# Odd head pairs on swapped halves of a bank of their own, and QK in 64x64 tiles

## The chip, the core and the metric

One core of a Trainium2 chip runs the whole program. The metric is device time in microseconds (us), from the first to the last instruction of one execution. Before the change it is 432.07 us, the median of three runs (430.96 to 432.35).

## What is computed

Three layers follow one another: decayed linear attention (retention), a soft mixture of experts, and a bilinear layer.

```python
scores = q @ k.T / sqrt(64)                    # 8 batches, 8 heads, 576 positions, 64 features
x = (scores * gamma_h ** (i - j) * (i >= j)) @ v   # -> 4608 tokens x 512 features
logits = x @ phi                               # 32 slots, 8 experts of 4
slots = softmax(logits, over tokens).T @ x     # 32 x 512
slot_out[e] = relu(slots[e] @ w1[e]) @ w2[e]   # 8 experts, 512 -> 1024 -> 512
x = softmax(logits, over slots) @ slot_out
out = (((x @ m1) * (x @ m2)) @ w3) @ w_out
```

## The kernel before

**Units.** The 4608 tokens are worked through as 36 units of 128 tokens. An item (g, c) takes the sequences g and g + 4 and 128 positions of each (c = 0 to 3); its two units, x = 0 and 1, are one sequence each. The item c = 4 is a single unit, the tail, with the last 64 positions of both sequences. So each of the four groups g has nine units: two with c = 0, six with c = 1 to 3, one tail.

**Heads.** A unit has four head pairs p. Pair p holds head h = 0 on SBUF partitions 0 to 63 (`lo`) and head h = 1 on partitions 64 to 127 (`hi`), with the 64 features along the partitions. The result `xts` has the same order: feature rows of pair p, tokens along the free axis.

**The steps of a unit on TensorE**, each a burst of fp32 matmuls. An fp32 matmul that isn't a transpose stands in the profile as two MATMUL records; "rows*columns" is the part of the 128x128 array that it takes.

- `emit_kt` (L201): four 128*128 transposes of the scaled keys into a miscellaneous bank; ScalarE copies it to `kt` (L202).
- `emit_qk` (L229): eight matmuls, 64*128, keys stationary, 128 query columns moving; head 0 goes to bank 0, head 1 to bank 1. The tail uses 64*64 (L224).
- `emit_p` on VectorE (L239, two instructions): bank 0 and 1 times the causal mask, into `pm`.
- `emit_pv` (L257): eight matmuls, 128*64, adding v x pm to the unit's result bank. The tail uses 64*64 (L250).
- `emit_state` (L270): eight matmuls, 128*64, adding k x v to the running state in bank 4; ScalarE copies it out after each item.
- `emit_inter` (L290): eight matmuls, 64*64, state x q, that start the unit's result bank; only where c > 0. In the tail sixteen, with 64 moving columns.
- `emit_xt` on VectorE (L303, L299 in the tail): the result bank times a table of decays, into `xts`.
- `emit_xtr` (L315): four transposes of `xts`, four units later; every fourth unit also `emit_logits` (L325, 16 matmuls, 128*32) and `emit_slots` (L409).

The result bank of a unit is whole: all four pairs, head 0 on partitions 0 to 63 and head 1 on 64 to 127, as the inputs lie. Odd and even units take turns between two banks:

```python
def xt_view(u):
    return bank[(5, 3)[u % 2]].rearrange("p (k t) -> p k t", k=4)
```

**Order.** Nothing is scheduled automatically; each engine runs its instructions in the order in which the loop writes them. Iteration u of the unit loop writes: key scaling for unit u + 4 (GpSimd L188, ScalarE L193), keys' transposes of u + 3, PV of u, state of u + 1, QK and mask of u + 2, `emit_xt` of u, inter of u + 1, next transfers, transposes of unit u - 4, softmax pieces, and between them the conversion of the weights of the last layer in five steps a piece (VectorE L465, L467, L459; ScalarE L464, L466; GpSimd L485). All transfers are issued by SyncE (SP) in program order; SP waits in order for a buffer to become free.

**Before the loop** SP issues the small tables and the first keys, queries and values (L609 to L621); `kr` are raw keys, scaled into `k`. VectorE L643 and GpSimd L649 build the decay tables from `xtab_sb` and `stab_sb`.

**After the loop** the buffers of the units are filled with expert weights (`in_ew`, 64 tiles of 512 KB, L544); the eight experts run on them (L553, L572) beside the product of w3 and w_out (L526). Then come the pairwise tables (L943) and the output stage (L1006 to L1011).

Of the kernel before, what the change touches and what calls it, by code (L numbers as in the profile page):

```python
# [31 lines left out]
def retention_softmoe_bilinear(  # L32
# [76 lines left out]
    even = tabs_sb[:, 196:197]  # L109
    ptail = tmp.tile([128, 256], F32, tag="h0", name="ptail").rearrange("p (k i) -> p k i", k=4)  # L110
# [96 lines left out]
    def xt_view(u):  # L207
        return bank[(5, 3)[u % 2]].rearrange("p (k t) -> p k t", k=4)
# [7 lines left out]
    def emit_qk(u):  # L216
        Q = q_tile(u)
        x = units[u][1]
        if tail(u):
            ps = qk_view(0).rearrange("p (x k i) -> p x k i", x=2, k=4)  # L220
            for x in range(2):
                for p in range(4):
                    for h, a in halves:
                        nc.tensor.matmul(out=ps[a, x, p], lhsT=Q[a, 1, x, p], rhs=Q[a, 0, x, p], start=True, stop=True)  # L224
            return
        for p in range(4):
            for h, a in halves:
                ps = qk_view(h).rearrange("p (k c i) -> p k c i", k=4, c=2)
                nc.tensor.matmul(out=ps[:, p], lhsT=ktb[u % 2][a, p], rhs=Q[a, :, x, p], start=True, stop=True)  # L229
# [13 lines left out]
    def emit_pv(u):  # L243
        x = units[u][1]
        if tail(u):
            V = vb[units[u][0] % VBUF][:, 0:512].rearrange("p (x k j) -> p x k j", x=2, k=4)
            for x in range(2):
                for p in range(4):
                    for h, a in halves:
                        nc.tensor.matmul(  # L250
                            out=xt_view(u)[a, p, 64 * x:64 * x + 64], lhsT=V[a, x, p], rhs=p_tail(u)[a, x, p],
                            start=False, stop=True, skip_group_check=True,
                        )
            return
        for p in range(4):
            for h, a in halves:
                nc.tensor.matmul(  # L257
                    out=xt_view(u)[a, p], lhsT=v_tile(u)[:, 1 - h, x, p], rhs=p_main(u)[:, h, p],
                    start=(block_of(u) == 0 and p == 0), stop=True, skip_group_check=True,
                )  # L260
# [21 lines left out]
    def emit_inter(u):  # L282
# [4 lines left out]
        for y in range(2) if tail(u) else (x,):  # L287
            for p in range(4):
                for h, a in halves:
                    nc.tensor.matmul(  # L290
                        out=xt_view(u)[a, p, 64 * y:64 * y + 64] if tail(u) else xt_view(u)[a, p].rearrange("p (c i) -> p c i", c=2),
                        lhsT=S[a, y, p], rhs=Q[a, 0, y, p] if tail(u) else Q[a, :, x, p],
                        start=(p == 0 and (y == 0 or not tail(u))), stop=True, skip_group_check=True,
                    )

    def emit_xt(u):
        v4 = lambda t: t.rearrange("p k (x i) -> p k x i", x=2)
        if tail(u):
            nc.vector.tensor_tensor(  # L299
                out=v4(xts[u % 6]), in0=v4(xt_view(u)), in1=xtab_sb[0][:, :, 0:64].unsqueeze(2).to_broadcast([128, 4, 2, 64]), op=ALU.mult,  # L300
            )
        else:
            nc.vector.tensor_tensor(out=xts[u % 6], in0=xt_view(u), in1=xtab_sb[block_of(u)], op=ALU.mult)  # L303
# [301 lines left out]
    with tc.manual_schedule():  # L605
# [9 lines left out]
        nc.sync.dma_start(out=xtab_sb[0][:, :, 0:64], in_=tabs[:, 328:584].rearrange("p (k i) -> p k i", k=4))  # L615
# [5 lines left out]
        nc.sync.dma_start(out=phi_sb, in_=phi)  # L621
# [7 lines left out]
        for n in (512, 512, 128):  # L629
# [14 lines left out]
            out=xtab_sb[0][:, :, 64:128], in0=xtab_sb[0][:, :, 0:64], in1=stab_sb[:, 1].unsqueeze(2).to_broadcast([128, 4, 64]), op=ALU.mult,  # L644
# [3 lines left out]
        for c in range(1, 4):  # L648
            nc.gpsimd.tensor_tensor(out=xtab_sb[c], in0=xtab_sb[0], in1=stab_sb[:, 2 * c].unsqueeze(2).to_broadcast([128, 4, 128]), op=ALU.mult)  # L649
# [17 lines left out]
        for u in range(NU):  # L667
# [11 lines left out]
            emit_pv(u)  # L679
            if u + 1 < NU:  # L680
# [4 lines left out]
            emit_xt(u)  # L685
# [93 lines left out]
        for k in range(4):  # L779
            nc.tensor.matmul(out=sT[:, k], lhsT=acc[:, 128 * k:128 * k + 128], rhs=ib, start=True, stop=True)  # L780
# [309 lines left out]
```

## Time and profile before

| | |
|---|---|
| median of three runs | 432.07 us |
| the profiled execution's own time | 432.36 us |
| its span (first to last instruction) | 430.6 us |
| TensorE matmul busy | 408.1 us, 95% of the span |
| VectorE, ScalarE, GpSimd busy | 57%, 46%, 39% |
| DMA | 47968 packets, 108.15 MB, 251 GB/s on average |
| granted TensorE clock | full from slice 1 to 40 |

Read it by stage: up to about 191 us the unit loop, from there to about 281 us the experts, then tables and the output stage. "Busy" counts a record from its modelled start to its modelled end, so a busy TensorE may still be filling, draining or running half of its array. Where a burst's length matters, take the distance from its start to the start of the next burst.

### The profile page before, as it was taken

The numbers are of one execution on the slowest core, as the hardware profiler recorded it, in microseconds if no ns is written. First come the engines' busy times: TensorE is split into PE (matmuls) and PEld (weight loads), VectorE is DVE, ScalarE is ACT, GpSimd is POOL, SyncE is SP. The second block draws the span as 40 slices with busy tenths as digits, with TensorE's granted clock in tenths as the row PEclk, the third lists the DMA queues.
The fourth block names the chain that finished last, engine by engine and source line by source line (L and its number), as shares of the span: only waits on it lengthen the run. The fifth ranks groups of instructions, "written<-read, shape, count | busy, mean of one in ns | idle before, by whom it ended". The sixth has DMA issues, their size and how long they took to land.

```text
span 430.6 us, 10442 instructions
## 1 busy us (share of the span) xinstructions
PE 408.1 (95%) x4211; PEld 312.0 (72%) x4211; DVE 246.2 (57%) x456; ACT 198.0 (46%) x415; POOL 166.6 (39%) x149
## 2 busy tenths in 40 slices
PE   5999898999899999999999988899999999999996
PEld 3888787888788777786556544356888888888884
DVE  3356677787677676654587556228964434443420
ACT  2233775665546555552455433123444445444431
POOL 0521666543425333431354333102745344434410
PEclk9999999999999999999999999999999999999999
DMA  5986798689677884869999999969054988879733
GB/s 157 362 298 241 259 330 287 178 286 349 241 221 244 294 282 161 299 198 352 393 354 413 408 410 408 401 166 189 1 132 89 231 216 201 209 198 231 188 79 93
DMA packets 47968, 108.15 MB, mean 251 GB/s; under 512 B 7376, under 2 KB 10064, under 8 KB 47920
## 3 DMA queue, kind: packets, MB, share of 16 engines
q1 hardware_dynamic: 47920, 107.49, 78.0%
q8 instruction: 33, 0.54, 0.5%
q14 instruction: 15, 0.12, 0.1%
HBM read 96.85 MB, written 10.62 MB: 250 GB/s over the span
## 4 chain that ended last, share of the span: by engine, by line
PE 76%; DMA 18%; ACT 2%; SPq 1%; DVE 1%; issue 1%; DVEq 0%; ACTq 0%
PE bank L229 9%; PE bank L1006 8%; PE bank L1007 8%; PE bank L1008 8%; PE bank L257 8%; DMA k<-in_ew 7%; PE bank L290 7%; DMA kt<-in_ew 5%; PE bank L943 5%; PE bank L201 4%; PE bank L315 4%; PE bank L270 4%; DMA v<-in_ew 2%; DMA xts<-in_ew 2%; PE bank L526 2%; PE bank L1009 2%
## 5 line engine op out<-in xcount | busy, mean ns | idle before, releaser
L597 POOL TENSOR_TENSOR cc<-mw_sb,cc 128x512 fp32r<-128x512 f32 x36 | 46.8, 1310 | 55.9 <-ACT cc L596 55.9
L239 DVE TENSOR_TENSOR pm<-bank,msb 128x512 f32<-128x512 f32 x64 | 41.2, 686 | 44.4 <-PE bank L229 44.4
L485 POOL TENSOR_TENSOR vals<-vals,msb 128x512 int32<-128x512 int32 x24 | 30.7, 1280 | 66.7 <-DVE vals L459 44.2
L526 PE MATMUL bank<-wop,w3p 128*128 128x512 f32 x192 | 50.4, 405 | 0.0
L595 DVE TENSOR_TENSOR mw_sb<-lga,raw 128x512 f32<-128x512 f32 x32 | 30.0, 958 | 35.3 <-POOL cc L597 28.0
L316 ACT COPY xg<-bank 128x512 f32<-128x512 f32 x34 | 20.0, 587 | 64.4 <-PE bank L315 64.4
L1011 ACT ACTIVATE mw_sb<-bank,rz 128x512 f32<-128x512 f32 x36 | 24.8, 689 | 49.8 <-PE bank L1009 28.6
L526 PEld LDWEIGHTS bank<-wop,w3p 128*128 128x128 f32 x192 | 34.2, 188 | 14.9 <-issue 8.7
L1006 PE MATMUL bank<-w3p,cc 128*128 128x512 f32 x108 | 42.4, 392 | 0.0
L1007 PE MATMUL bank<-w3p,cc 128*128 128x512 f32 x108 | 42.2, 391 | 0.0
L1008 PE MATMUL bank<-w3p,cc 128*128 128x512 f32 x108 | 42.2, 391 | 0.0
L229 PE MATMUL bank<-q,kt 64*128 64x128 f32 x512 | 39.6, 295 | 0.8 <-DVE pm L239 0.8
L485 POOL TENSOR_TENSOR mw_sb<-mw_sb,msb 128x512 int32<-128x512 int32 x16 | 20.3, 1270 | 47.7 <-DVE mw_sb L459 24.5
L229 PEld LDWEIGHTS bank<-q,kt 64*128 64x128 f32 x512 | 33.2, 196 | 3.8 <-DVE pm L239 1.1
L257 PE MATMUL bank<-pm,v 128*64 128x128 f32 x512 | 35.0, 279 | 0.0
L495 POOL TENSOR_TENSOR w3p<-vals,w3p 128x512 fp32r<-128x512 f32 x16 | 20.5, 1282 | 33.8 <-ACT w3p L490 33.8
L257 PEld LDWEIGHTS bank<-pm,v 128*64 128x64 f32 x512 | 27.3, 136 | 5.4 <-issue 5.4
L188 POOL TENSOR_TENSOR k<-kr,msb 128x512 f32<-128x512 f32 (+1 forms) x30 | 24.4, 835 | 17.6 <-DMA kr<-in_v 14.3
L290 PE MATMUL bank<-q,st 64*64 64x128 f32 (+1 forms) x512 | 30.6, 261 | 0.0
L201 PE MATMUL bank<-cst,k 128*128 128x128 f32 x128 | 21.4, 294 | 8.5 <-ACT lga L352 6.8
L466 ACT ACTIVATE msb<-raw 128x512 int32<-128x512 uint32 x40 | 27.8, 696 | 0.0
L596 ACT CAST cc<-mw_sb 128x512 fp32r<-128x512 f32 x36 | 21.6, 618 | 13.0 <-DVE mw_sb L595 10.4
(191 smaller groups left out, 784.1 us busy)
## 6 DMA issues: line engine op xcount, KB each, us to landing
q<-in_q SPq DMA_DIRECT2D x20, 512.0 KB, 5.6
raw<-expt SPq DMA_DIRECT2D x36, 256.0 KB, 4.4
kr<-in_v SPq DMA_DIRECT2D x16, 512.0 KB, 5.0
v<-in_v SPq DMA_DIRECT2D x16, 512.0 KB, 6.1
raw<-in_m SPq DMA_DIRECT2D x16, 512.0 KB, 6.2
raw<-in_w SPq DMA_DIRECT2D x16, 512.0 KB, 6.0
out_x<-mw_sb SPq DMA_DIRECT2D x64, 128.0 KB, 2.7
k<-in_ew SPq DMA_DIRECT2D x14, 512.0 KB, 10.2
```

The source lines that it names most:

```text
L201: nc.tensor.transpose(ps[:, 128 * p:128 * p + 128], k_tile(u)[:, x, p].rearrange("p h j -> p (h j)"), ident)
L229: nc.tensor.matmul(out=ps[:, p], lhsT=ktb[u % 2][a, p], rhs=Q[a, :, x, p], start=True, stop=True)
L239: nc.vector.tensor_tensor(out=p_main(u)[:, h], in0=qk_view(h).rearrange("p (k t) -> p k t", k=4), in1=mask_sb.unsqueeze(1).to_broadcast([1 ...
L257: nc.tensor.matmul(out=xt_view(u)[a, p], lhsT=v_tile(u)[:, 1 - h, x, p], rhs=p_main(u)[:, h, p], start=(block_of(u) == 0 and p == 0), stop ...
L290: nc.tensor.matmul(out=xt_view(u)[a, p, 64 * y:64 * y + 64] if tail(u) else xt_view(u)[a, p].rearrange("p (c i) -> p c i", c=2), lhsT=S[a, ...
L485: nc.gpsimd.tensor_tensor(out=ti, in0=ti, in1=parts[j % 2].bitcast(I32), op=ALU.add)
L526: nc.tensor.matmul(out=ps, lhsT=x, rhs=y, start=(k8 == 0 and part == 0), stop=(k8 == 7 and part == 2))
L595: eng.tensor_tensor(out=e, in0=x, in1=y[:, m], op=ALU.mult)
L597: nc.gpsimd.tensor_tensor(out=cl[m], in0=e, in1=ch[m], op=ALU.subtract)
L1006: nc.tensor.matmul(out=ob, lhsT=ch[m][:, sl], rhs=gh[m], start=(m == 0), stop=False)
L1007: nc.tensor.matmul(out=ob, lhsT=ch[m][:, sl], rhs=gl[m], start=False, stop=False)
L1008: nc.tensor.matmul(out=ob, lhsT=cl[m][:, sl], rhs=gh[m], start=False, stop=False)
```

## The change

Heads of odd pairs (p = 1, 3) now leave TensorE on the other half of the partitions, into bank 3, and even pairs go to bank 5, in every unit. So the 64x64 tiles of `emit_inter` (and of the tail's PV) use, in turn, all four quarters of the array: rows lo to columns lo, hi to hi, lo to hi, hi to lo. `emit_qk` is cut into twice as many matmuls, each with 64 of the 128 key columns, in the same four quarters. Both result banks are used by each unit, so `emit_xt` becomes two VectorE instructions of half the size and stands straight behind PV. What depends on the row order of odd pairs follows: the decay table, a second position table `xstab`, `phi`, and the slots' transposition `sT`.

```diff
+    xstab = tabs_sb[:, 200:236].rearrange("p (c k) -> p c k", c=9)
-    def xt_view(u):
-        return bank[(5, 3)[u % 2]].rearrange("p (k t) -> p k t", k=4)
+    def xt_view(p):
+        return bank[(5, 3)[p % 2]][:, 128 * (p // 2):128 * (p // 2) + 128]
+
+    def side(p, h):
+        return (lo, hi)[h ^ (p % 2)]
...
-                nc.tensor.matmul(out=ps[:, p], lhsT=ktb[u % 2][a, p], rhs=Q[a, :, x, p], start=True, stop=True)
+                for b in (lo, hi):
+                    nc.tensor.matmul(out=ps[b, p], lhsT=ktb[u % 2][a, p, b], rhs=Q[a, :, x, p], start=True, stop=True)
...
-                    out=xt_view(u)[a, p], lhsT=v_tile(u)[:, 1 - h, x, p], rhs=p_main(u)[:, h, p],
-                    start=(block_of(u) == 0 and p == 0), stop=True, skip_group_check=True,
+                    out=xt_view(p)[side(p, h)], lhsT=v_tile(u)[:, 1 - h, x, p], rhs=p_main(u)[:, h, p],
+                    start=(block_of(u) == 0 and p < 2), stop=True, skip_group_check=True,
...
     def emit_xt(u):
...
+        for r in range(2):
+            ps = bank[(5, 3)[r]][:, 0:256].rearrange("p (k t) -> p k t", k=2)
+            o, f = xts[u % 6][:, r::2], xtab_sb[block_of(u) % 4][:, r::2]
...
+            nc.vector.tensor_tensor(out=o, in0=ps, in1=f, op=ALU.mult)
...
-        nc.sync.dma_start(out=xtab_sb[0][:, :, 0:64], in_=tabs[:, 328:584].rearrange("p (k i) -> p k i", k=4))
+        for r in range(2):
+            for a, b in ((lo, hi), (hi, lo)) if r else ((slice(0, 128),) * 2,):
+                nc.sync.dma_start(out=xtab_sb[0][a, r::2, 0:64], in_=tabs[b, 328:584].rearrange("p (k i) -> p k i", k=4)[:, r::2])
+                nc.sync.dma_start(out=xstab[a, :, r::2], in_=tabs[b, 292:328].rearrange("p (c k) -> p c k", c=9)[:, :, r::2])
...
-        nc.sync.dma_start(out=phi_sb, in_=phi)
+        for r in range(2):
+            for a, b in ((lo, hi), (hi, lo)) if r else ((slice(0, 128),) * 2,):
+                nc.sync.dma_start(out=phi_sb[a, r::2], in_=phi[b, r::2])
...
             emit_pv(u)
+            emit_xt(u)
             if u + 1 < NU:
                 emit_state(u + 1)
             if u + 2 < NU:
                 emit_qk(u + 2)
                 emit_p(u + 2)
-            emit_xt(u)
             if u + 1 < NU:
                 emit_inter(u + 1)
...
         for k in range(4):
-            nc.tensor.matmul(out=sT[:, k], lhsT=acc[:, 128 * k:128 * k + 128], rhs=ib, start=True, stop=True)
+            for a, b in ((lo, 64), (hi, 0)) if k % 2 else ((slice(0, 128), 0),):
+                n = a.stop - a.start
+                nc.tensor.matmul(out=sT[a, k], lhsT=acc[:, 128 * k + b:128 * k + b + n], rhs=ib, start=True, stop=True)
```

The tables that `emit_xt` and the loops before it read come from `xstab` in place of `stab_sb`; the line numbers of the changed kernel are a few higher (QK L234, inter L295, PV L262, state L275, mask L244, `emit_xt` L308).

TensorE before, one iteration of the loop with c > 0, from the keys' transposes on (bank_67 and bank_68 are banks 0 and 1, bank_72 is bank 5, bank_70 bank 3, bank_71 the state):

```order
L201 MATMUL bank_69<-cst,k_111 128x128 x4
L257 MATMUL bank_72<-pm_97,v_105 64x128 x8
L270 MATMUL bank_71<-v_105,k_110 64x64 x8
L229 MATMUL bank_67<-q_103,kt 128x128
L229 MATMUL bank_68<-q_103,kt 128x128
...
L290 MATMUL bank_70<-q_102,st 64x128 x8
L201 MATMUL bank_73<-cst,k_109 128x128 x4
L257 MATMUL bank_70<-pm_98,v_105 64x128 x8
```

The same iteration of the changed kernel:

```order
L202 MATMUL bank_69<-cst,k_111 128x128 x4
L262 MATMUL bank_72<-pm_97,v_105 64x128 x2
L262 MATMUL bank_70<-pm_97,v_105 64x128 x2
...
L275 MATMUL bank_71<-v_105,k_110 64x64 x8
L234 MATMUL bank_67<-q_103,kt 64x128 x2
L234 MATMUL bank_68<-q_103,kt 64x128 x2
...
L295 MATMUL bank_72<-q_102,st 64x128 x2
L295 MATMUL bank_70<-q_102,st 64x128 x2
...
L202 MATMUL bank_73<-cst,k_109 128x128 x4
```

QK stands as 16 matmuls in place of eight, and inter writes both result banks, where before it wrote the bank that the unit ahead of it had not used.

VectorE before, from the mask of one unit to the mask of the next, in an iteration with logits:

```order
L239 TENSOR_TENSOR pm_98<-bank_67,msb 128x512
L239 TENSOR_TENSOR pm_98<-bank_68,msb 128x512
L303 TENSOR_TENSOR xts_92<-bank_70,xtab_84 128x512
L465 TENSOR_SCALAR mw_sb<-mw_sb 128x512
L331 TENSOR_REDUCE mt<-bank_69 128x1
L336 TENSOR_TENSOR mn<-mt,mn 128x1
L338 TENSOR_SCALAR nm<-mn 128x1
L467 TENSOR_SCALAR mw_sb<-mw_sb 128x512
L459 SCALAR_TENSOR_TENSOR mw_sb<-raw,mw_sb 128x512
L239 TENSOR_TENSOR pm_97<-bank_67,msb 128x512
```

and of the changed kernel:

```order
L308 TENSOR_TENSOR xts_92<-bank_72,xtab_84 128x2x128
L308 TENSOR_TENSOR xts_92<-bank_70,xtab_84 128x2x128
L244 TENSOR_TENSOR pm_98<-bank_67,msb 128x512
L244 TENSOR_TENSOR pm_98<-bank_68,msb 128x512
L470 TENSOR_SCALAR mw_sb<-mw_sb 128x512
L336 TENSOR_REDUCE mt<-bank_69 128x1
...
L464 SCALAR_TENSOR_TENSOR mw_sb<-raw,mw_sb 128x512
L308 TENSOR_TENSOR xts_93<-bank_72,xtab_84 128x2x128
L308 TENSOR_TENSOR xts_93<-bank_70,xtab_84 128x2x128
L244 TENSOR_TENSOR pm_97<-bank_67,msb 128x512
```

The two halves of `emit_xt` moved from behind the mask to ahead of it, and so behind the conversion steps of the unit before.

SP before, from the first values to the second keys (msb holds the position tables, slotm the decay table):

```order
L177 DMA v_104<-in_v 128x2x512
L615 DMA slotm<-in_tabs 128x4x64
L161 DMA kr_108<-in_v 128x2x512
```

and of the changed kernel:

```order
L178 DMA v_104<-in_v 128x2x512
L622 DMA slotm<-in_tabs 128x2x64
L623 DMA msb<-in_tabs 128x18x1
L622 DMA slotm<-in_tabs 64x2x64
L623 DMA msb<-in_tabs 64x18x1
L622 DMA slotm<-in_tabs 64x2x64
L623 DMA msb<-in_tabs 64x18x1
L162 DMA kr_108<-in_v 128x2x512
```

Six table transfers stand where one did; a "18x1" one consists of single fp32 elements.

## Rows read from the trace of the kernel before

**Rows 1.** Stretches: TensorE, its loads, VectorE, ScalarE, GpSimd, clock, DMA share, GB/s

```profile
10.80:24.60 13.80, 13.02 (x159) 11.53 (x158) 6.08 (x9) 4.21 (x10) 8.01 (x9) 1.00 1.02 331
80.00:100.00 20.00, 20.00 (x346) 16.98 (x346) 15.96 (x29) 12.46 (x30) 9.48 (x9) 1.00 0.71 239
220.00:240.00 20.00, 20.00 (x158) 10.79 (x156) 14.82 (x35) 8.12 (x18) 9.48 (x8) 1.00 1.02 400
```

**Rows 2.** The page's chain that ended last, by engine

```profile
PE 76%; DMA 18%; ACT 2%; SPq 1%; DVE 1%; issue 1%; DVEq 0%; ACTq 0%
```

**Rows 3.** The same chain in order of time, from the loop's last units on

```profile
190.59 1.10 PE bank L250 x32
192.09 8.73 DMA k<-in_ew
200.88 9.46 DMA xts<-in_ew
```

**Rows 4.** TensorE in order of time: start, us, instruction, count

```profile
83.42 1.09 PE L290 MATMUL bank<-q,st 64*64 64x128 f32 x16
84.45 0.66 PE L315 MATMUL bank<-cst,xts 128*128 128x128 f32 x4
85.03 1.08 PE L325 MATMUL bank<-xts,cst 128*32 128x128 f32 x32
86.04 1.09 PE L257 MATMUL bank<-pm,v 128*64 128x128 f32 x16
86.97 0.63 PE L270 MATMUL bank<-v,k 128*64 128x64 f32 x16
87.53 1.16 PE L229 MATMUL bank<-q,kt 64*128 64x128 f32 x16
88.62 1.09 PE L290 MATMUL bank<-q,st 64*64 64x128 f32 x16
```

**Rows 5.** TensorE around a tail's QK

```profile
92.15 1.15 PE L224 MATMUL bank<-q 64*64 64x64 f32 x32
93.14 1.04 PE L290 MATMUL bank<-q,st 64*64 64x128 f32 x16
94.11 0.66 PE L315 MATMUL bank<-cst,xts 128*128 128x128 f32 x4
```

**Rows 6.** VectorE in order of time, the stretch of rows 4

```profile
83.53 1.29 DVE L239 TENSOR_TENSOR pm<-bank,msb 128x512 f32<-128x512 f32 x2 [1.22 <-PE bank L229]
84.73 0.68 DVE L303 TENSOR_TENSOR xts<-bank,xtab 128x512 f32<-128x512 f32 x1
85.33 1.49 DVE L465 TENSOR_SCALAR mw_sb<-mw_sb 128x512 f32<-128x512 f32 x1
...
87.77 0.69 DVE L459 SCALAR_TENSOR_TENSOR mw_sb<-raw,mw_sb 128x512 uint32<-128x512 uint32 x1
```

**Rows 7.** VectorE groups by form: busy us, mean ns

```profile
L857 DVE COPY acc<-bank 128x256 f32<-128x256 f32 x1 | 0.4, 424 | 5.0 <-ACT acc L856 5.0
```

**Rows 8.** All engines in order of time, start of the loop

```profile
13.85 1.79 POOL L188 TENSOR_TENSOR k<-kr,msb 128x512 f32<-128x512 f32 x2 [11.59 <-DMA kr<-in_v]
...
17.36 1.52 PE L201 MATMUL bank<-cst,k 128*128 128x128 f32 x8
```

**Rows 9.** Source lines L177 and L615, first issue of each: start, issue to landing

```profile
L177 SPq DMA_DIRECT2D v<-in_v x1: 607/607/607, 5.9 to 5.9; - x1
...
DMA to landing us min/median/max: 6.0/6.0/6.0
...
L615 SPq DMA_DIRECT2D slotm<-in_tabs x1: 604/604/604, 6.6 to 6.6; - x1
...
DMA to landing us min/median/max: 5.8/5.8/5.8
```

**Rows 10.** Transfers by line: issues, size of each, median us to landing

```profile
msb<-in_tabs SPq DMA_DIRECT2D x4, 4.0 KB, 2.3
...
expt<-et SPq DMA_DIRECT2D x8, 16.0 KB, 1.6
```

More of the change, by code (lines that the diff above doesn't have):

```diff
@@ L250, in emit_pv @@
                         nc.tensor.matmul(
-                            out=xt_view(u)[a, p, 64 * x:64 * x + 64], lhsT=V[a, x, p], rhs=p_tail(u)[a, x, p],
+                            out=xt_view(p)[side(p, h), 64 * x:64 * x + 64], lhsT=V[a, x, p], rhs=p_tail(u)[a, x, p],
                             start=False, stop=True, skip_group_check=True,
@@ L290, in emit_inter @@
                     nc.tensor.matmul(
-                        out=xt_view(u)[a, p, 64 * y:64 * y + 64] if tail(u) else xt_view(u)[a, p].rearrange("p (c i) -> p c i", c=2),
+                        out=xt_view(p)[side(p, h), 64 * y:64 * y + 64] if tail(u) else xt_view(p)[side(p, h)].rearrange("p (c i) -> p c i", c=2),
                         lhsT=S[a, y, p], rhs=Q[a, 0, y, p] if tail(u) else Q[a, :, x, p],
-                        start=(p == 0 and (y == 0 or not tail(u))), stop=True, skip_group_check=True,
+                        start=(p < 2 and (y == 0 or not tail(u))), stop=True, skip_group_check=True,
                     )
     def emit_xt(u):
[L297 to L303, printed above, removed]
+        for r in range(2):
+            ps = bank[(5, 3)[r]][:, 0:256].rearrange("p (k t) -> p k t", k=2)
+            o, f = xts[u % 6][:, r::2], xtab_sb[block_of(u) % 4][:, r::2]
+            if tail(u):
+                o, ps = (t.rearrange("p k (x i) -> p k x i", x=2) for t in (o, ps))
+                f = f[:, :, 0:64].unsqueeze(2).to_broadcast([128, 2, 2, 64])
+            nc.vector.tensor_tensor(out=o, in0=ps, in1=f, op=ALU.mult)
     L = {"cc": []}
@@ L643, in retention_softmoe_bilinear @@
         nc.vector.tensor_tensor(
-            out=xtab_sb[0][:, :, 64:128], in0=xtab_sb[0][:, :, 0:64], in1=stab_sb[:, 1].unsqueeze(2).to_broadcast([128, 4, 64]), op=ALU.mult,
+            out=xtab_sb[0][:, :, 64:128], in0=xtab_sb[0][:, :, 0:64], in1=xstab[:, 1].unsqueeze(2).to_broadcast([128, 4, 64]), op=ALU.mult,
         )
@@ L648, in retention_softmoe_bilinear @@
         for c in range(1, 4):
[L649 removed]
+            nc.gpsimd.tensor_tensor(out=xtab_sb[c], in0=xtab_sb[0], in1=xstab[:, 2 * c].unsqueeze(2).to_broadcast([128, 4, 128]), op=ALU.mult)
         emit_qk(1)
```

## The prediction

> **What bounds the kernel now.** I read the stretches first, then the chain of waits, then both engines' order of time inside one unit, and last the start, where the change adds transfers.
>
> In the unit loop TensorE is never idle: 20.00 of 20 us from 80 to 100 us, at a granted clock of 1.00, while the DMA share is 0.71 [rows 1]. After the loop the limit is another one: from 220 to 240 us the DMA share is 1.02 at 400 GB/s. The chain says the same, TensorE with 76% and DMA with 18% of the span [rows 2]; its first long DMA pieces begin at 192.09 us, right behind the loop's last burst at 190.59 [rows 3], because those expert tiles go into buffers that the loop gives back at its end. So what the loop saves moves the whole expert stream forward, and I carry it to the end at full value.
>
> **How long a burst takes, and why.** The distance between the starts of two bursts is what counts [rows 4]. PV, 16 records with 128 columns on two column halves, takes 86.04 to 86.97 = 0.93 us; state, the same shape with 64 columns, 0.56; QK 87.53 to 88.62 = 1.09; inter 83.42 to 84.45 = 1.03. Two records run side by side, so PV is eight steps. Four unknowns fit all of these: a step of 128 columns, 0.109 us; one of 64 columns, 0.058; a first weight load, 0.05, which nothing covers; and 0.10 for emptying the array where the next burst has another tile shape. PV: 8 x 0.109 + 0.05 = 0.92, with no change of shape before state. State: 8 x 0.058 + 0.10 = 0.56. Inter: 0.87 + 0.05 + 0.10 = 1.02. QK's 128-column loads make its first load 0.12. The proof of the last term is the tail: its QK has inter's shape, and there inter takes 93.14 to 94.11 = 0.97 in place of 1.03, and QK itself 0.99 = 16 x 0.058 + 0.05, without the 0.10 [rows 5].
>
> **The change, part by part.**
>
> *Inter.* Eight matmuls of 128 columns on two quarters are eight steps; on four quarters four steps. No row shows four quarters at once. The nearest rows show each half of it: PV runs two column halves on the same rows side by side, QK two row halves, and logits (L325) four column strips, 32 records in 1.01 us, eight steps [rows 4]. I take four at a time. Inter then costs 4 x 0.109 + 0.10 = 0.54. Of 24 full inters 20 stand behind a full QK: 1.03 - 0.54, and as the first load now hides behind QK of the same shape, I count 0.48 each; 4 stand behind a tail's QK, 0.97 - 0.54 = 0.43. Together 9.6 + 1.7 = 11.3 us.
>
> *QK.* Twice the matmuls, half the columns, four at a time: still eight steps. It gains the smaller first load (0.07), and 0.10 more where inter follows in the same shape. That is 23 units x 0.17 and 9 x 0.07, 4.5 us.
>
> *Tails.* Four inters of 16 x 0.058 + 0.15 = 1.08 would become 8 x 0.058 + 0.10 = 0.56, four PVs (1.10 [rows 3]) 0.61: 4 x 0.52 + 4 x 0.49 = 4.0 us if records can start every 15 ns. The fastest long burst shown is logits, 0.109 / 4 = 27 ns a record; at that rate 32 records still take 0.87 and the gain is 0.6 us. I take 2.2, about the middle.
>
> Sum for TensorE: 18.0 us, between 16.4 and 19.8 by the tails.
>
> *A new wait.* Inter of unit u + 1 now writes the banks that `emit_xt` of u reads; before, they alternated. So VectorE has to reach `emit_xt` and finish it before QK of u + 2 ends. Two 128x256 instructions take 0.424 us each [rows 7], overlapping by the 0.08 that the two mask instructions show (1.29 for two of 0.69 [rows 6]): 0.76 us against 0.68 today. Behind inter stand the transposes and PV, so all of TensorE waits. Walk through the stretch shown: the mask starts at 83.53, and without L303 behind it L465 (1.49 us here) starts 0.6 earlier, so the last conversion step ends at 87.77 + 0.69 - 0.6 = 87.86 and `emit_xt` at 88.6. QK would start 0.48 earlier than 87.53, last 0.92 and end at 87.97: inter is 0.6 us late. That is a unit with logits and a slow L465; a unit has spare time otherwise, for VectorE has 4 us of 20 idle [rows 1]. I count four such units, 2.5 us, with 0 and 28 x 0.3 = 8.4 as ends.
>
> *The start.* The six table transfers contain 2304 + 2 x 1152 = 4608 pieces of 4 bytes, ahead of the second keys, queries and values. The DMA engines are full there, share 1.02 [rows 1]. Nothing shows 4-byte pieces. One end: the decay table's 512 pieces of 256 bytes, issued at 6.6, landed at 12.4, behind the values at 5.9 + 6.0 = 11.9, so 0.5 us, 1.0 ns a piece [rows 9]: 4.6 us. The other: 256 pieces of 16 bytes land in 2.3 us, where another small transfer of 32 pieces lands in 1.6 [rows 10]; 0.7 us / 224 is 3.1 ns a piece: 14.4 us. The first is nearer in load, the second in size; I take 1.2 ns, 5.5 us, as full queues are what the new pieces meet. GpSimd waits for exactly these keys (11.59 us, until 13.85) and has them scaled at 15.64; TensorE transposes them at 17.36 [rows 8]. So 1.7 us are spare, and 3.8 are a stall, once: later loads are two and three items ahead. Ends 1 and 12.7. SP's five further issues of 0.6 us run under the queue's backlog, for the values take 6.0 us from issue to landing [rows 9].
>
> *At no cost.* `phi` in three pieces is needed 25 us later. The two extra matmuls of `sT` come while the chain waits for expert tiles (192 to 210 us [rows 3]); without that cover they cost about 0.1 us.
>
> **Sum.** 18.0 - 2.5 - 3.8 = 11.7 us. The profiled execution took 432.36 us, 0.29 more than the median; against the median I predict 420.4 us.
>
> **Rivals.**
>
> *Slower: weight loads of two quarters on the same rows do not run beside a matmul on those rows.* Then a step is 0.109 + 0.05 = 0.16. QK becomes 1.33 (1.43 with emptying): 23 x 0.24 + 9 x 0.34 = 8.6 us lost; inter 0.74: 24 x 0.29 = 7.0 won. With the start's 3.8 that is 5.4 us more, 437.5 us. The change loses from a step of 0.145 us on. For it speaks that no row has four quarters. Against it: PV's two column halves share all rows and still step in 0.109 [rows 4]. [...] 10%.
>
> *VectorE paces the loop.* Between 80 and 100 us it is busy 15.96 of 20 [rows 1]; with 0.08 more a unit and the loop a tenth shorter that is over 90%, in strict order, with two waits for TensorE in each unit. If each of 28 inters comes 0.3 late: 420.4 + 5.9 = 426.3 us. 10%.
>
> *The start is dear.* At 3.1 ns a piece: 432.07 - 18.0 + 2.5 + 12.7 = 429.3 us. 10%.
>
> **How the numbers follow.** The forecast itself has 70%. Its best corner is 19.8 won, 1 lost at the start and none on VectorE, 413.3 us; its poor one 16.4 won, 7.5 and 5 lost, 428.2. The range 413.3 to 428.5 holds nearly all of it and VectorE's rival; it leaves out the slower rival and half of the dear start. About 0.3% (1.3 us) is what a measurement of this kernel can tell from no change. Faster by more: the forecast and two rivals, less the meeting of two poor cases, 0.87. Slower: 0.10. Between: 0.03.
>
> **What would show it.** Inter's bursts 0.54 us apart from the next, QK 0.92 before inter. About 512 more MATMUL records. The packet count up by some 5000. TensorE's transposes of the second keys at about 21 us in place of 17.36. A new line in the waits: TensorE's inter behind `emit_xt`, a few us in all, mostly in units with logits. The expert stream full from about 180 us, and the stage behind the loop as long as before. It is wrong if QK's bursts grow beyond 1.1 us, if inter waits in every unit, or if the loop ends 12 us earlier and the experts do not.

## The result, and the profile after

The changed kernel takes 425.92 us (425.62 to 430.72 in four runs) where the kernel before, on the same chip, takes 431.67 (430.96 to 432.35): a ratio of 0.9891, with an interval of 0.9856 to 0.9926. It is faster, by 5.75 us. 420.4 us were forecast, so a little less than half of the forecast gain of 11.7 us came.

The profiled execution took 425.71 us, with a span of 424.0 where before it was 430.6. The page's first and third parts, and its row of the granted clock:

```profile
PE 393.7 (93%) x4727; PEld 297.3 (70%) x4727; DVE 252.0 (59%) x492; ACT 198.2 (47%) x415; POOL 167.6 (40%) x149
PEclk9589999999999999999999999999999999999999
DMA packets 53076, 108.24 MB, mean 255 GB/s; under 512 B 12608, under 2 KB 15168, under 8 KB 53024
q8 instruction: 37, 0.61, 0.6%
```

TensorE has 516 records more and the queues 5108 packets more than before, as announced. In the row of the clock the second of the forty slices (10.6 to 21.2 us) fell to 0.5 and the third to 0.8. The last row is a queue that the forecast never looked at: TensorE's instructions, 37 fetches of 16 KB, before 33.

The stretches of [rows 1], now:

```profile
10.80:24.60 13.80, 9.10 (x104) 7.55 (x106) 3.48 (x7) 1.30 (x4) 4.60 (x5) 0.51 0.82 197
80.00:100.00 20.00, 19.54 (x403) 15.64 (x396) 17.07 (x36) 12.54 (x30) 10.65 (x10) 1.00 0.80 252
220.00:240.00 20.00, 20.00 (x152) 12.07 (x151) 12.25 (x31) 9.33 (x22) 8.30 (x7) 1.00 1.02 407
```

Three readings. In the start TensorE does 9.10 us of work instead of 13.02, and its granted clock is 0.51 instead of 1.00. That figure alone doesn't give TensorE's speed there: the first two QKs take 2.08 and 2.67 us in the kernel before, at 1.00, and 1.99 and 2.57 now, at 0.50; later ones take 1.16 and 1.10. In the loop VectorE went from 15.96 to 17.07 of 20, and TensorE now idles 0.46 us. Behind the loop nothing changed.

An undisturbed unit is what the forecast said. TensorE in order of time (start, duration), as in [rows 4]:

```profile
29.43 1.10 PE L234 MATMUL bank<-q,kt 64*64 64x128 f32 x32
30.35 0.62 PE L295 MATMUL bank<-q,st 64*64 64x128 f32 x16
30.90 0.66 PE L202 MATMUL bank<-cst,k 128*128 128x128 f32 x4
```

QK to inter is 0.92, inter to the next burst 0.55; 0.92 and 0.54 were forecast. The whole unit, from one PV's start to the next, takes 3.55 us, before 4.19. Around a tail, the counterpart of [rows 5]:

```profile
55.60 0.64 PE L295 MATMUL bank<-q,st 64*64 64x64 f32 x32
56.17 0.66 PE L320 MATMUL bank<-cst,xts 128*128 128x128 f32 x4
...
57.30 0.69 PE L255 MATMUL bank<-pm,v 64*64 64x64 f32 x32
57.93 0.69 PE L275 MATMUL bank<-v,k 128*64 128x64 f32 x16
```

32 small matmuls in 0.57 and in 0.63 us, 18 to 20 ns each. The forecast had hesitated between 15 and 27 ns and had taken half of the tails' gain; all of it came.

So where did five microseconds go? First, the start. Before (see also [rows 8]), the issues of the second and third keys and unit 1's PV:

```profile
7.21 0.61 SPq L161 DMA_DIRECT2D kr<-in_v  x1
...
11.97 0.64 SPq L161 DMA_DIRECT2D kr<-in_v  x1
...
21.97 1.09 PE L257 MATMUL bank<-pm,v 128*64 128x128 f32 x16
```

Now, all engines in order of time:

```profile
7.86 4.10 SPq L622 DMA_DIRECT2D slotm<-in_tabs  x1
...
14.07 0.72 SPq L162 DMA_DIRECT2D kr<-in_v  x1
...
19.43 1.61 POOL L189 TENSOR_TENSOR k<-kr,msb 128x512 f32<-128x512 f32 x2 [17.18 <-DMA kr<-in_v]
20.25 0.63 SPq L162 DMA_DIRECT2D kr<-in_v  x1
21.10 1.97 PE L202 MATMUL bank<-cst,k 128*128 128x128 f32 x8 [3.84 <-POOL k L189]
23.00 1.79 PE L262 MATMUL bank<-pm,v 128*64 128x128 f32 x16
27.35 0.66 PE L202 MATMUL bank<-cst,k 128*128 128x128 f32 x4 [1.07 <-POOL k L189]
27.94 1.09 PE L262 MATMUL bank<-pm,v 128*64 128x128 f32 x16
```

SP asks for the second keys at 14.07 us where it was 7.21 before: one issue behind the first four-byte pieces alone holds it for 4.10 us. The third keys are asked for at 20.25, before at 11.97. TensorE waits 3.84 us, transposes them and does unit 0's PV at a granted clock of 0.50 (the PV lasts 1.79 instead of 1.09), then waits again for the third keys. Unit 1's PV starts 5.96 us late. The clock didn't fall behind this wait: it was granted at 0.50 from between 10 and 11 us to between 24 and 25 us, and the long wait begins at 17.26 only. A run below with the same start (the thin steps) shows 1.00 in its place (columns as in [rows 1]):

```profile
10.80:24.60 13.80, 10.05 (x113) 8.17 (x113) 4.07 (x8) 1.60 (x4) 4.61 (x5) 1.00 0.86 213
```

The bursts are no shorter there: QK takes 1.99 and 2.56 us, the second keys' transposes 1.97, unit 0's PV 1.98. Unit 1's PV starts at 27.32 instead of 27.94, and GpSimd starts on the third keys at 25.07 instead of 25.68: those 0.6 us come with the keys. A price of the granted clock isn't shown in this start.

Second, a unit with logits, TensorE and then VectorE in the same stretch (before: [rows 4] and [rows 6]):

```profile
87.73 1.10 PE L234 MATMUL bank<-q,kt 64*64 64x128 f32 x32
89.30 0.98 PE L295 MATMUL bank<-q,st 64*64 64x128 f32 x16 [0.46 <-DVE xts L308]
90.22 0.55 PE L320 MATMUL bank<-cst,xts 128*128 128x128 f32 x3
```

```profile
86.71 0.95 DVE L341 TENSOR_TENSOR mn<-mt,mn 128x1 f32<-128x1 f32 x1
...
87.77 0.42 DVE L472 TENSOR_SCALAR mw_sb<-mw_sb 128x512 uint32<-128x512 uint32 x1
88.22 0.69 DVE L464 SCALAR_TENSOR_TENSOR mw_sb<-raw,mw_sb 128x512 uint32<-128x512 uint32 x1
88.83 0.74 DVE L308 TENSOR_TENSOR xts<-bank,xtab 128x256 f32<-128x256 f32 x2
```

PV ended long before; VectorE reaches the scaling at 88.83 only, behind the logits' maximum and two conversion steps, and inter stands for it. Its 16 records then also take 0.92 from start to start instead of 0.55: they write the two banks in turn, and VectorE has read the second one only at 89.57 (88.83 + 0.74). The costliest case is the last tail's inter, which has no QK ahead of it to cover anything:

```profile
180.37 1.09 PE L262 MATMUL bank<-pm,v 128*64 128x128 f32 x16
182.16 0.75 DVE L308 TENSOR_TENSOR xts<-bank,xtab 128x256 f32<-128x256 f32 x2
182.72 1.01 PE L295 MATMUL bank<-q,st 64*64 64x64 f32 x32 [1.26 <-DVE xts L308]
```

PV and this inter take 3.29 us from PV's start on, where undisturbed they need 1.02 + 0.57: 1.7 us lost in one place.

Behind the loop the rest is carried over as forecast: the expert tiles' stream ends earlier by about as much as the loop, its last long piece in the chain before and now are these two, and the span is shorter by 6.6.

```profile
271.28 9.45 DMA k<-in_ew
```

```profile
264.54 9.46 DMA k<-in_ew
```

The account, from the distances between starts of bursts, unit by unit, up to the PV of the last unit (35; before, it starts at 190.52, the burst at the head of [rows 3]), which starts 6.27 us earlier than before:

```profile
184.25 0.69 PE L255 MATMUL bank<-pm,v 64*64 64x64 f32 x32
```

```
                         forecast   measured
TensorE, undisturbed      -18.0      -18.8
start                      +3.8       +6.0
inter behind VectorE       +2.5       +5.0   (nine units; 1.7 in the last)
TensorE stops mid-burst      -        +1.2   (see the last experiment section)
smaller ones                 -        +0.3
sum                       -11.7       -6.3
```

Of the 1.2 us of stops 0.4 lie in unit 3's PV, 0.5 in unit 4's QK and 0.3 in the logits behind unit 9's PV.

### The profile page after: what moved, and what is told of

It is laid out like the page before. It is cut to its first block, busy times and chain, and to the rows that moved or that the text cites. A ratio compares the mean times of both kernels' runs of the same rounds, so it can differ in the third digit from the quotient of the medians.

```text
span 424.0 us, 11525 instructions
## 1 busy us (share of the span) xinstructions
PE 393.7 (93%) x4727; PEld 297.3 (70%) x4727; DVE 252.0 (59%) x492; ACT 198.2 (47%) x415; POOL 167.6 (40%) x149
## 4 chain that ended last, share of the span: by engine, by line
PE 38%; DMA 10%; DVE 1%; ACT 1%; SPq 1%; issue 0%; ACTq 0%
PE bank L1018 8%; PE bank L1019 8%; PE bank L1020 8%; PE bank L955 5%; DMA k<-in_ew 5%; PE bank L531 3%; DMA kt<-in_ew 2%; DMA v<-in_ew 2%; PE bank L1021 2%; PE bank L577 2%; PE bank L558 1%; DMA lga<-expt 1%; PE bank L979 1%; DVE w L540 0%; SPq L592 0%
## 5 line engine op out<-in xcount | busy, mean ns | idle before, releaser
L244 DVE TENSOR_TENSOR pm<-bank,msb 128x512 f32<-128x512 f32 x64 | 41.2, 684 | 16.9 <-PE bank L234 16.9
L234 PE MATMUL bank<-q,kt 64*64 64x128 f32 x1024 | 38.3, 285 | 1.1 <-DVE pm L244 0.8
L262 PE MATMUL bank<-pm,v 128*64 128x128 f32 x512 | 36.0, 283 | 0.1
L189 POOL TENSOR_TENSOR k<-kr,msb 128x512 f32<-128x512 f32 (+1 forms) x30 | 25.4, 866 | 23.5 <-DMA kr<-in_v 23.5
L500 POOL TENSOR_TENSOR w3p<-vals,w3p 128x512 fp32r<-128x512 f32 x16 | 20.5, 1283 | 33.6 <-ACT w3p L495 33.6
L234 PEld LDWEIGHTS bank<-q,kt 64*64 64x64 f32 x1024 | 29.7, 138 | 4.6 <-DVE pm L244 1.5
L262 PEld LDWEIGHTS bank<-pm,v 128*64 128x64 f32 x512 | 28.1, 139 | 5.9 <-issue 5.6
L202 PEld LDWEIGHTS bank<-cst,k 128*128 128x128 f32 x128 | 14.8, 146 | 17.9 <-ACT lga L357 6.3
```

The source lines that it names most:

```text
L202: nc.tensor.transpose(ps[:, 128 * p:128 * p + 128], k_tile(u)[:, x, p].rearrange("p h j -> p (h j)"), ident)
L234: nc.tensor.matmul(out=ps[b, p], lhsT=ktb[u % 2][a, p, b], rhs=Q[a, :, x, p], start=True, stop=True)
L244: nc.vector.tensor_tensor(out=p_main(u)[:, h], in0=qk_view(h).rearrange("p (k t) -> p k t", k=4), in1=mask_sb.unsqueeze(1).to_broadcast([1 ...
L262: nc.tensor.matmul(out=xt_view(p)[side(p, h)], lhsT=v_tile(u)[:, 1 - h, x, p], rhs=p_main(u)[:, h, p], start=(block_of(u) == 0 and p < 2), ...
```

## Experiments on the start

The theory was two mis-sized terms, the start and VectorE's queue. The rivals: the transfers' share (up to 0.94 in the loop), or a gain of QK's split that is waited away.

**The four-byte pieces alone, in the kernel before** (at the same place of SP's queue, into unused columns):

```diff
+        for r in range(2):
+            for a, b in ((lo, hi), (hi, lo)) if r else ((slice(0, 128),) * 2,):
+                nc.sync.dma_start(out=spare[a, :, r::2], in_=tabs[b, 292:328].rearrange("p (c k) -> p c k", c=9)[:, :, r::2])
```

> The kernel before, with the three transfers of four-byte pieces of the changed kernel put at the same place of SP's queue, into columns that nobody reads. Theory (the start costs 6.0 us because SP and the rings are held by these pieces before the second keys are asked for): SP's issue of the second keys moves from 7.21 to about 12.5 us, they are transposed at about 20.5 instead of 17.36, and the kernel takes 4.5 to 6 us longer, 436 to 438. Rival (the pieces are cheap and the late start comes from the other added transfers, the split table of 256 columns, or from QK's 32 instructions): under 2 us longer, second keys before 18.5 us.

436.41 us against 431.8, a ratio of 1.0106 (1.0086 to 1.0126). All engines in order of time:

```profile
7.21 5.56 SPq L619 DMA_DIRECT2D msb<-in_tabs  x3
...
12.81 0.87 SPq L161 DMA_DIRECT2D kr<-in_v  x1
...
19.92 1.97 PE L201 MATMUL bank<-cst,k 128*128 128x128 f32 x8 [2.10 <-POOL k L188]
```

Three issues hold SP for 5.56 us, the second keys are asked for 5.6 us late, and from unit 1 to unit 35 every PV starts 4.83 us late, to within 0.01. A delay of the start is neither made up in the loop nor behind it. The pieces are 4.8 of the start's 6.0 us.

**The small table as whole rows** (no four-byte pieces, one small copy on VectorE):

```diff
-                nc.sync.dma_start(out=xstab[a, :, r::2], in_=tabs[b, 292:328].rearrange("p (c k) -> p c k", c=9)[:, :, r::2])
+                if r:
+                    nc.sync.dma_start(out=xstab[a], in_=tabs[b, 292:328].rearrange("p (c k) -> p c k", c=9))
...
+        nc.vector.tensor_copy(xstab[:, :, 0::2], stab_sb[:, :, 0::2])
```

> The changed kernel, with the second scale table fetched as whole rows of 144 bytes (two transfers, halves swapped) and its even columns copied on VectorE: no four-byte pieces left, two issues fewer on SP less one. Theory: second keys issued at about 10 us instead of 14.07, transposed at about 18 to 19 instead of 21.10, the clock not lowered behind it, and 4 to 6 us off the end, 420 to 422. Rival (VectorE's queue in the loop sets the pace, so that an earlier start is lost again in its waits): 424 to 426.

423.4 us, a ratio of 0.9797 (0.9764 to 0.9829): 2.5 us off the changed kernel, half of what was expected. (Here and below such differences are between medians of kernels that weren't measured side by side; the kernel before, measured beside each, took 431.67 to 432.34 us.) The second keys came in time (PV of unit 0 starts at 18.55, even before the 18.81 of the kernel before), but the third were asked for at 16.34 instead of 11.97, behind the split tables and `phi`'s three issues, and TensorE waits for them:

```profile
23.64 0.66 PE L202 MATMUL bank<-cst,k 128*128 128x128 f32 x4 [2.49 <-POOL k L189]
```

Unit 1's PV starts 2.25 us later than in the kernel before, and from there to unit 2's it takes 5.13 us instead of 3.55, at a granted clock of 0.50 from 25 to 27 us. What the pieces don't cost, the other transfers that were added on SP do.

**The same transfers behind the second item's:**

```diff
         load_v(0)
-        for r in range(2):
...
-                nc.sync.dma_start(out=xstab[a, :, r::2], in_=tabs[b, 292:328].rearrange("p (c k) -> p c k", c=9)[:, :, r::2])
         load_k(1)
         load_q(1)
         load_v(1)
+        for r in range(2):
...
+                nc.sync.dma_start(out=xstab[a, :, r::2], in_=tabs[b, 292:328].rearrange("p (c k) -> p c k", c=9)[:, :, r::2])
```

> The changed kernel with the same small table transfers, four-byte pieces included, but asked for behind the second keys, queries and values. Theory (it is the place ahead of the second keys in SP's queue that costs): second keys issued at about 7 us and transposed at about 17.4 as before; the tables' product on VectorE, which stands ahead of the second mask, then waits to about 19 us, so PV of unit 0 comes about 2 us late instead of 4.2; 3 to 6 us off the end, 420 to 423. Rival (the pieces hold the rings wherever they stand): third keys and values late instead, under 2 us off, 424 to 426.

428.09 us, 0.9927 (0.9903 to 0.9951): the interval overlaps the changed kernel's, but in the trace the last unit's PV comes 3.8 us later than there. No gain in any case, a miss of the theory as it was put. The second keys were indeed in time, but now the third stood behind the pieces: asked for at 22.47 us, transposed at 29.44 after a wait of 5.1. Whoever stands behind the pieces pays for them.

**The tables on ScalarE's queue**, whole rows, before the first keys; SP's queue keeps the keys, queries and values (`phi` moves too, in the same way; the small copy on VectorE as above):

```diff
         load_k(0)
+        for r in range(2):
+            for a, b in ((lo, hi), (hi, lo)) if r else ((slice(0, 128),) * 2,):
+                nc.scalar.dma_start(out=xtab_sb[0][a, r::2, 0:64], in_=tabs[b, 328:584].rearrange("p (k i) -> p k i", k=4)[:, r::2])
+                if r:
+                    nc.scalar.dma_start(out=xstab[a], in_=tabs[b, 292:328].rearrange("p (c k) -> p c k", c=9))
+        for a, b in ((lo, hi), (hi, lo)):
+            nc.scalar.dma_start(out=ptail[a], in_=tabs[b, 0:256].rearrange("p (k i) -> p k i", k=4))
...
         nc.sync.dma_start(out=cst[:, 0:160], in_=consts)
```

> The changed kernel with the tables of the start, whole rows instead of four-byte pieces, asked for by ScalarE's queue while ScalarE waits for the first keys, so that SP's queue has the keys, queries and values alone. Theory (the start's 6 us are SP's queue): second keys issued at 6.6 us, third near 10, unit 1's PV at about 21.5 to 22.5 instead of 27.94, and 5.5 to 7 us off the changed kernel, 419 to 420.5. Rival (the start is bound by what the rings can move, and VectorE's loop eats what is left): under 3 us off, 423 to 426.

420.36 us, 0.9749 (0.9713 to 0.9785): 5.6 us off the changed kernel, as expected. Unit 1's PV starts at 21.89, before 21.97; the start's whole price, 6.05 us, is gone there. Not all of it arrives: from unit 1's PV to the last one this run takes 158.03 us, the changed kernel 156.31, for it stops longer in the middle of bursts (see the last experiment section). On the whole rows on SP's queue it gains 2.3 us at unit 1 (24.22 to 21.89).

## Experiments on VectorE

**VectorE's conversion steps cut to 32 of 512 columns, in the changed kernel and in the kernel before:**

```diff
-            lambda: v.tensor_scalar(out=t, in0=t, scalar1=W_MIN, ...
+            lambda: v.tensor_scalar(out=t[:, 0:32], in0=t[:, 0:32], scalar1=W_MIN, ...
```

(and likewise in the other two steps)

> The changed kernel with VectorE's three steps of the weight conversion on 32 of their 512 columns, which leaves out most of the conversion of the last layers' weights there (ScalarE's and GpSimd's steps stay). Theory (about 7 us of the gain are lost in the loop because the two scalings stand behind these steps on VectorE): the unit's time comes down to 3.5 us in nearly all units, inter's waits on the scaling go, the last PV comes 6 to 8 us earlier than in the changed kernel, and 5 to 8 us come off the end, 418 to 421. Rival (the transfers, at up to 0.94 of their capacity, or the clock set the pace in the loop): under 1.5 us off, over 424.

> The kernel before, with VectorE's three steps of the weight conversion on 32 of their 512 columns, as in the run of the changed kernel with thin steps (most of the conversion is left out). Theory (only the changed kernel has inter waiting for the scaling, so only there do these steps cost TensorE): within 1 us of the kernel before, 431 to 432.5. Rival (VectorE's work paces the loop of either kernel): 2.5 to 4 us off, about 428, like the 3.8 us that they gave in the changed kernel.

Changed kernel: 422.08 us, 0.9776 (0.9754 to 0.9799), 3.8 us off. Kernel before: 431.33 against 432.34, 0.9978 (0.9958 to 0.9999), and in the trace each of its PVs from unit 0 to 35 starts at the same distance, +0.27. So VectorE's load costs TensorE something in the changed kernel only, and in the way named; but the amount expected for the changed kernel (5 to 8 us) was too high. The 3.8 us are not VectorE's price alone: in the trace the last PV comes 3.4 us earlier than in the changed kernel, of which 0.6 are there at unit 1 already and come with the third keys; from unit 1 to unit 35 the loop takes 153.56 us in place of 156.31, although this run's stops in the middle of bursts are longer by about 1 us. So of the 5.0 us behind VectorE about 4 go; what stays is above all the last tail's inter (1.0 of its 1.7). The rival of the transfers falls too, for their share stays (0.95 from 60 to 80 us) while the time goes.

TensorE's waits in the changed kernel with thin steps, from 24 to 182 us (us in total, times, longest):

```profile
PE bank L202 <- ACT lga L357: 6.8, 5, 1.5
PE bank L320 <- issue: 0.9, 1, 0.9
PE bank L234 <- issue: 0.6, 1, 0.6
PE bank L295 <- DVE xts L308: 0.5, 1, 0.5
```

The first is there in the kernel before with the same 6.8. The two with "issue" are new and no semaphore explains them.

**The scaling at its old place, behind the mask:**

```diff
             emit_pv(u)
-            emit_xt(u)
             ...
                 emit_p(u + 2)
+            emit_xt(u)
```

> The changed kernel with the scaling of unit u again behind the mask of unit u+2 on VectorE, where the kernel before has it. Theory (a single pair of banks makes inter wait for the scaling, so its place decides): every inter then waits for QK, the mask's 1.28 us and the scaling's 0.83, some 1.5 to 2 us in each of 28 units; the loop loses 30 to 50 us, of which the units' other waits hide little: 455 to 475. Rival (the scaling's place hardly matters, VectorE's total decides): 425 to 430.

495.33 us, a ratio of 1.1448 (1.1391 to 1.1504), worse than expected. TensorE's waits of the whole execution, and the stretch from 60 to 80 us (columns as in [rows 1]):

```profile
PE bank L295 <- DVE xts L308: 45.3, 28, 1.8
```

```profile
60.00:80.00 20.00, 15.96 (x277) 12.74 (x273) 8.47 (x18) 9.34 (x23) 9.11 (x9) 0.79 0.51 163
```

All 28 inters wait, 1.6 us each. Most of the rest of the loss goes, by estimate, with the granted clock, 0.79 in this stretch where TensorE is busy 15.96 of 20 us, and 0.946 over the whole execution where the changed kernel has 0.984. The move of `emit_xt` ahead of QK, a line of the diff that looks like housekeeping, is what makes the change possible at all.

**Another order on VectorE**: the last two steps of a weight piece run behind the next unit's scaling, where VectorE waits for QK anyway.

```diff
-            next_conv(u - 2)
-            run_conv(1)
             ...
             emit_xt(u)
+            run_conv(2)
+            run(adds)
+            next_conv(u - 2)
+            run_conv(1)
             ...
-            run_conv(1)
+            run_conv(2)
             ...
-            run_conv(4)
```

> The changed kernel with the same work and another order on VectorE: the last two steps of a weight piece run behind the next unit's scaling instead of ahead of it, where VectorE waits for QK anyway. Theory (it is the place ahead of the scaling, not the amount of VectorE's work): inter's waits shrink in the units with logits and with slots, 1.5 to 3.5 us off the changed kernel, 422.5 to 424.5. Rival (VectorE is simply full there): 425 to 427.

424.98 us (422.63 to 426.36), 0.9824 (0.9775 to 0.9873): its interval overlaps the changed kernel's, so the time alone doesn't decide. The trace does. From unit 6 to unit 35 the loop takes 132.93 us where the changed kernel takes 136.04, 3.1 less, with nearly all waits of inter gone. What eats it is one stop in unit 4's QK, in TensorE's order of time:

```profile
40.04 0.88 PE L234 MATMUL bank<-q,kt 64*64 64x128 f32 x22
43.15 0.54 PE L234 MATMUL bank<-q,kt 64*64 64x128 f32 x9 [2.23 <-issue]
```

```profile
42.00:44.00 2.00, 0.85 (x26) 0.84 (x26) 0.35 (x1) 0.00 (x0) 0.00 (x0) 1.00 0.09 33
44.00:46.00 2.00, 2.00 (x24) 1.67 (x20) 1.27 (x3) 1.14 (x3) 0.00 (x0) 0.72 0.23 60
```

TensorE stops in the middle of a burst, with no semaphore to wait for and with nearly idle DMA engines (share 0.09 from 42 to 44 us), and its granted clock is lower behind it (0.72 from 44 to 46 us).

**One scaling instruction for both banks** (put next to each other):

```diff
+    two = psum.tile([128, 1024], F32, name="two")
...
+            nc.vector.tensor_tensor(out=kr(xts[u % 6]), in0=ps, in1=kr(xtab_sb[block_of(u)]), op=ALU.mult)
```

> The changed kernel with the two banks of the pairs next to each other, so that one instruction of 512 columns scales both (tail units keep two). Per unit 0.68 us instead of 0.83 on VectorE, 5 us of VectorE's time in the whole loop; but inter's first half then waits for all of the scaling. Theory (a wait counts only where the scaling ends late): 0 to 1.5 us off, 424.4 to 426. Rival (VectorE's amount of work paces the loop): 3 to 5 us off, 421 to 423.

431.55 us, 0.9993 (0.9965 to 1.0021). For the total this is inconclusive: with the two banks in one tile, the last stage, far behind the loop, takes new waits (four, 3.3 us in all, for ScalarE's copies), which is not all of the 5 us that come on top behind the loop. In the loop the last unit's PV starts at 184.09, in the changed kernel at 184.25: 5 us less of work on VectorE are worth 0.2 on TensorE. That speaks against the rival that VectorE's sum paces the loop.

## QK's split by itself

```diff
-                nc.tensor.matmul(out=ps[:, p], lhsT=ktb[u % 2][a, p], rhs=Q[a, :, x, p], ...)
+                for b in (lo, hi):
+                    nc.tensor.matmul(out=ps[b, p], lhsT=ktb[u % 2][a, p, b], rhs=Q[a, :, x, p], ...)
```

Alone in the kernel before:

> The kernel before with QK alone split: 32 instructions of 64 rows of output instead of 16 of 128, nothing else changed (no tables, no second bank, inter in two quarters on its single bank). Theory: 0.17 us off each QK that inter follows, 4 to 4.5 us in the loop, all carried to the end because nothing new is waited for, 427 to 428.5; of that up to 1 us may be lost to TensorE idling in the middle of a burst without a releaser, which the kernel before never shows and which would be its instructions arriving late (a fetch of 16 KB every 6 to 7 us instead of 8). Rival (the split only moves work into waits): 430.5 to 432.

And taken back in the changed kernel:

> The changed kernel with QK's 16 instructions of 128 rows of output as before, the state times q still in all four quarters. Theory: a QK takes 1.09 again instead of 0.92 and the step from QK to the inter is back; 4.5 us lost on TensorE, of which 1 to 2 come back because VectorE has that much more time per unit and TensorE fetches fewer instructions (no idle time in the middle of a burst without a releaser): 428 to 430. Rival (the split of QK earns nothing, its gain is waited away elsewhere): 425 to 427.

Alone it gives 4.9 us: 426.87 against 431.76, 0.9893 (0.9878 to 0.9907). TensorE's order of time there:

```profile
26.61 1.10 PE L230 MATMUL bank<-q,kt 64*64 64x128 f32 x32
27.53 1.05 PE L291 MATMUL bank<-q,st 64*64 64x128 f32 x16
```

0.92 to inter, and no semaphore is newly waited for in the loop; 4.6 of it are in the loop, although unit 4's QK loses 0.4 us in the middle of the burst, which its expectation had allowed for. Taken back, it costs less than it gives alone: 427.63 us, 0.9898 (0.987 to 0.9926), which is not to be told from the changed kernel's ratio; in the trace the last PV comes 2.2 us later, and the loop from unit 1 to unit 35 takes 3.0 us longer (159.30). Both theories' values were missed by a little: part of QK's gain is lost again in the changed kernel, behind VectorE and in TensorE's stops, but not all. Its expectation that TensorE would no longer stop in a burst fell: there is one such stop, 0.45 us in the logits at 104.1 us.

Here lies the plainest reading of the result: one line of the diff, with no table, no bank and no wait for VectorE, gives 4.9 of the change's 5.75 us, by the ratios (0.9893 and 0.9891) not to be told from the whole change. The inter in four quarters earns over 13 us on TensorE and pays nearly all of it back.

## Both repairs, and TensorE's stops

ScalarE's queue for the tables, and the other order on VectorE:

> The same start together with the other order on VectorE (the last two steps of a weight piece behind the next unit's scaling). Theory (start and VectorE's order are two separate terms and add up): another 2.5 to 3.5 us off, 416 to 418; TensorE's stop of 2.2 us in the fifth unit's QK, which the reordered run showed with the rings full, should be gone with the crowding of the start. Rival (they share one cover): as the run with the start alone, 419 to 421.

417.7 us (415.77 to 419.63), 0.9678 (0.9642 to 0.9714): better than both kernels, 8.2 us below the changed one. The two terms nearly add up (5.6 and 3.1). The unit with logits of above, TensorE and VectorE in order of time:

```profile
82.18 1.09 PE L262 MATMUL bank<-pm,v 128*64 128x128 f32 x16
...
83.67 1.10 PE L234 MATMUL bank<-q,kt 64*64 64x128 f32 x32
84.59 0.62 PE L295 MATMUL bank<-q,st 64*64 64x128 f32 x16
```

```profile
83.10 0.76 DVE L308 TENSOR_TENSOR xts<-bank,xtab 128x256 f32<-128x256 f32 x2
83.78 1.27 DVE L472 TENSOR_SCALAR mw_sb<-mw_sb 128x512 uint32<-128x512 uint32 x1
```

The scaling starts as PV ends, the slow conversion step lies beside QK and inter, and inter waits for nothing. The expectation that unit 4's stop would go with the crowded start fell: it is still there, 1.1 us. And in this run the granted clock was 0.50 from 11 to 21 us (0.63 on average from 10.8 to 24.6), though the transfers of the start are those of the run with the start alone, which shows 1.00 there. Unit 1's PV starts at 23.28 instead of 21.89; how much of that is the clock isn't shown, for the first two QKs take 1.99 and 2.57 us in the run with the start alone, too.

These are the clearest of the stops, one or two of a trace: gaps between two records of the same burst, with the number of TensorE's records (loads, matmuls and semaphore instructions) before the gap.

```
kernel                         at us   stop in       records before
changed                        35.6    unit 3's PV         705
another order on VectorE       40.7    unit 4's QK         961
tables on ScalarE's queue      34.7    unit 4's QK         961
both repairs                   36.2    unit 4's QK         961
pieces behind the second item  69.2    logits             1985
tables on ScalarE's queue      80.4    logits             2753
thin steps                    100.5    a transposition    3520
whole rows                    137.7    inter              5057
```

The distances are 256, 1024, 768, 767 and 1537: multiples of 256, to within one record. A fetch of the instruction queue is 16 KB (37 for 0.61 MB), and to each come about 256 of TensorE's matmuls and loads (9454 for 37 fetches, 8422 for 33 in the kernel before): the stops lie whole fetches apart. The stop of the run with QK taken back fits too (3009, that is 256 behind 2753). TensorE has 37 such fetches instead of 33, and in the loop one about every 6 us instead of every 8.

The traces' DMA records of that queue show when the fetches ran. In the loop of the kernel before, each fetch starts at least 4.6 us before TensorE reaches the first record behind the next border. At the eight stops of the table the fetch starts late, and TensorE goes on 2.3 to 2.9 us after its start: in the reordered run the fetch starts at 40.5 us and QK goes on at 43.15, in the changed kernel at 33.6 and PV goes on at 36.00. No border is passed sooner than 2.2 us after its fetch's start in any of these runs. So at the stops TensorE seems to have run ahead of its own instructions, an inference from these times. There the fetch starts 3.4 to 5.0 us after the border before it, in the loop of the kernel before never more than 3.0; why it starts late in one place and not in another isn't shown.

## Why the prediction was right or wrong

**Right: the model of TensorE's steps.** 18.8 us of undisturbed gain against 18.0, burst by burst to 0.02 us, and four quarters at once, for which no row had stood. The rival that weight loads on the same rows don't overlap would have shown QK at 1.33; it shows 0.92. The tails were under-sized (all 4 us came instead of 2.2).

**Right: carried over.** The loop's 6.3 us are the span's 6.6.

**Wrong: the start, by its sentence "a stall, once: later loads are two and three items ahead".** The first stall was right almost to the digit: the second keys were 5.6 us late (forecast 5.5), transposed at 21.10 (about 21). In part that is luck, for the 1.2 ns a piece were picked between 1.0 and 3.1. But SP's queue is in order, so the third keys were late as well, 8.3 us at the issue, and made a second wait, of 1.07 us. 6.0 in place of 3.8. The sentence that SP's further issues run under the queue's backlog was wrong too: without the pieces the added transfers still cost 2.25 us at unit 1.

**Wrong: the wait for the scaling, by its count.** The mechanism, its place and the 0.6 us of a unit with logits were right (1.0 and 0.5 in two of them). But only three units behind logits waited, one of them the last tail, which has no QK to hide behind and was not thought of: 1.7 us. Six others waited without logits, by 0.1 to 0.5 us. In unit 16 two conversion steps were slow (0.89 and 0.72 us), but in units 25, 32 and 33 the three took their shortest times (0.42, 0.43 and 0.69). So "a unit has spare time otherwise" was wrong. 5.0 in place of 2.5. The rival "VectorE paces the loop" gave 426.3 us, close to the result, by the wrong way: not each inter came 0.3 us late but nine, by up to 1.7; and less work behind the scaling's place (one instruction for both banks) gave 0.2 us, while less work or another order ahead of it gave 3 to 4.

**Missing: TensorE's own instructions.** Doubling QK's matmuls was counted as free, since they take no more steps. TensorE's stops at the borders of its fetches cost about 1.2 us; not all of it is due to QK, for a stop is there with QK taken back as well.

## What to carry to other kernels

When a change makes an engine faster, look at three queues that had slack: the in-order queue that frees its results, the in-order queue that issues its loads, and its own instructions. Here the first and the last lost it to the faster engine, the second to the transfers that the change added (4.8 us in the kernel before, too). Price a small transfer not by its bytes but by what stands behind it in the issuing queue, and follow that queue for more than one step. And where a single-buffered result replaces an alternating one, look at what stands ahead of the reader in its queue, above all in the units where nothing covers it; moving work behind the reader gave 3 us in the loop.

## What was not expected of the hardware

SP was held 4.10 us by the issue behind the first 2304 four-byte pieces, and 5.56 by three such. TensorE's granted clock stood at 0.50 in the start of some executions and not in others with the same transfers: in the changed kernel it fell at about 11 us, behind a wait of 2.01 us (from 6.93 on) and ahead of the one of 3.84, in the run with thin steps it shows 1.00 behind waits of 2.17 and 2.96 us, yet the first two QKs take 1.99 and 2.57 us in the one and 1.99 and 2.56 in the other. In the reordered run it was 0.72 from 44 to 46 us, behind a stop of 2.23 us. What makes it fall, these runs don't show. And TensorE stopped in the middle of bursts, for 2.23 us in the reordered run (with the DMA engines at a share of 0.09 from 42 to 44 us), at places that lie multiples of 256 of its records apart, and went on 2.3 to 2.9 us after the start of a fetch.
